# The order of the head in a one-core FFT mixing and expert routing kernel: o tiles, blank places, SyncE's queue, comparisons on GpSimd

## The chip, the core and the metric

The kernel runs on one core of a Trainium2 chip. A core has five engines with instruction streams of their own: TensorE (PE, with its weight loads shown as PEld), VectorE (DVE), ScalarE (ACT), GpSimd (POOL) and SyncE (SP), which here only issues transfers. Each engine works through its stream in order and waits at an instruction until what it needs has been signalled. The metric is the device time of one launch in microseconds; the number that counts is the median of several runs.

## What is computed

The input x has 8 batches of 2496 rows with 256 columns. Each batch goes through a real FFT along its rows, a multiplication with a filter and the inverse FFT. The 19968 resulting rows are tokens; each goes through the expert that a hash of its number names.

```python
def _attn_ref(x, filt_r, filt_i):
    X = np.fft.rfft(x, axis=1)
    F = (filt_r + 1j * filt_i)[None, :, :]
    y = np.fft.irfft(X * F, n=x.shape[1], axis=1)
    return y.astype(np.float32)

def _moe_ref(x, token_ids, w1, w2):          # E = 8 experts, D = 256, F = 1024
    expert_idx = token_ids * np.int64(2654435761) % np.int64(E)
    for e in range(E):
        mask = expert_idx == e
        h = np.maximum(x[mask] @ w1[e], 0.0)
        out[mask] = h @ w2[e]
```

## The kernel before

**FFT.** A batch of 2496 = 39 x 64 rows is transformed in three stages: DFTs of length 39 (stage 1), products with twiddles, the filter and back (stage 2, in 10 steps `u`, plus one that only finishes the last), and DFTs of length 39 again (stage 3). A step of stage 2 is `forward` (matmul pb on PE, then the products y and z on DVE: L263, L266 twice, L267) and, one step later, `back` or `back_c` (matmul pc on PE, copied by ACT). For batches 0 and 1 everything stays on the chip: `stage1_c` (L309), `turn2` (transposes, L319), `back_c` (L330), `turn4` (transposes, L345, the copy L349) and `stage3` (matmul pd, L219; copy to an o tile, L221). Batches 2 to 7 pass through DRAM between the stages: `stage1` writes d1 from ACT's queue (L242), `load2` reads it back in five groups of two transfers (L248).

**Routing.** The number of a token gives its expert at once, and from that its place in `xs`, a DRAM buffer of 163 tiles of 128 places, ordered so that each tile holds tokens of one expert. `count` and `route` work out the running numbers, `later(g)` for g = 1, 2, 3 compares them with the stages' limits (8 comparisons L544 and an addition L546 each), `places` sums them (L550), writes them to DRAM and reads them back as indices `sidx`. `tile_experts` and `experts` work out which expert each tile has; `weights` needs that (`chunk_i`). `blanks` works out the places that no token takes (at most 127 in an expert) and scatters rows of a blank tile to them (7 indirect transfers).

**Stage 3 and the scatter.** One call of `stage3` makes an o tile of up to four groups of rows, and each group goes out as one indirect transfer of POOL (`scatter`, L376), 22 for a batch. Before the copies DVE writes the token's number into the o tile (L363). The pool of o tiles has two buffers.

**Experts.** `step(i)` of the loop: gather tile i + 4 (L696, from SP), `up` (32 matmuls L715, relu on ACT and DVE into ht), fetch the next weights, `turn(i + 1)` (transposes L704, copy L706 on DVE), then the pieces of the FFT of later batches that are due, `down` (16 matmuls L727, copy L730), and the scatter of the results to the output (L731, POOL). The tiles fall into four stages; those of stage g hold tokens of batches below 2, 4, 6 and 8 only, so that the loop starts when batches 0 and 1 are in `xs`. What comes before the loop is called the head here.

**Order.** The order is written out by hand: `todo` is a list of pairs of a due time and a piece of work. It is sorted by due time; pieces below 0 make up the head, and pieces from 0 on run inside the step with that number. The due times are only an order: each engine receives its instructions in the order in which the pieces are called.

**Memory shared by turns.** `load1` puts x tiles 0 to 3 (batch 0's three, batch 1's first) into the quarters of the tile `wts`, all others into a pool of two buffers (tag x). `wts` later holds the weights of two experts (w1 and w2 of each in a quarter), and its first two and a half quarters hold batch 0's values between stage 2 and `turn4`. `rpool`, the routing's pool, is closed before the pools of the expert loop (`gath`, `work`, `outs`) are opened, so they take its room. `ppool` (tag p) has four buffers for y and z, given out in turn; `t4pool` has two.

Of the kernel before, what the change touches and what calls it, by code (L numbers as in the profile page):

```python
# [11 lines left out]
F32 = mybir.dt.float32  # L12
# [103 lines left out]
def kernel(  # L116
# [40 lines left out]
    chunk_i = keep.tile([1, 2, NT], I32)  # L157
    used_i = keep.tile([1, 1], I32)
    wf_t = cpool.tile([NR, NK], F32)
    wi_t = cpool.tile([NK, NR], F32)  # L160
# [15 lines left out]
    class Batch:  # L176
# [14 lines left out]
        def load1(self, v):  # L191

            k = self.b * NV + v
            if k < 4:
                xt = wts[0:NR, k, :].rearrange("p (j c) -> p j c", c=C)
            else:
                xt = xpool.tile([NR, XL, C], F32, name=f"x_{self.b}_{v}", tag="x")
            self.x[v] = xt

            n = min(XL, HN + 1 - XL * v)  # L200
            for h in range(H):
                nc.sync.dma_start(out=xt[h:NR:H, 0:n, :],
                                  in_=bass.AP(tensor=x.tensor, offset=x.offset + (self.b * S + H0[h] + XL * v) * C,
                                              ap=[[N2 * C, N1], [C, n], [1, C]]))
# [154 lines left out]
        def stage3(self, u):  # L359

            n = min(XG, HN + 1 - XG * u)
            o = opool.tile([NR, XG, W], F32, name=f"o_{self.b}_{u}", tag="o")
            nc.vector.tensor_scalar(o[:, 0:n, C:].bitcast(I32),  # L363
                                    tokno[:, XG * u:XG * u + n].unsqueeze(2).to_broadcast([NR, n, W - C]),
                                    float(self.b * S), None, op0=OP.add)
            v, half = divmod(u, XL // XG)

            copy = nc.scalar.copy if self.b < 2 else nc.vector.tensor_copy
            self.products(wi_t, (NK, 2 * NS), N1, self.t4[v][:, half * XG:half * XG + XG, :], o, copy, u, "pd")
            for i in range(n):  # L370
                j = XG * u + i
                r = NR if j < HN else N1
                scatter(o[0:r, i, :], sidx[0:r, self.b, j:j + 1], f"xs_{self.b}")
# [30 lines left out]
    rctx = ctx.enter_context(ExitStack())  # L404
    rpool = pool(rctx, "route", 1)
    nc.sync.dma_start(out=wf_t[:], in_=wf_dram.ap())
    for v in range(NV):
# [57 lines left out]
    def count():  # L465
# [4 lines left out]
        nc.vector.tensor_copy(eid[:], eid_i[:])  # L470
        mask = rpool.tile([P, E, NJ], F32)
        nc.vector.tensor_tensor(mask[:], eid[:].unsqueeze(1).to_broadcast([P, E, NJ]),
                                over(iota_e[:], NJ), op=OP.is_equal)
        maskf = mask[:].rearrange("p e j -> p (e j)")
        run = rpool.tile([P, E, NJ], F32)
# [18 lines left out]
    def route():  # L494
# [35 lines left out]
        nc.vector.tensor_scalar(thr[:], full[:, 0:G, :], float(TB), 1.0, op0=OP.mult, op1=OP.add)  # L530
        acc = rpool.tile([P, E, NJ], F32)
        tmp = mask
# [8 lines left out]
    def later(g):  # L541
        acc, tmp, run = rv["acc"], rv["tmp"], rv["run"]
        for e in range(E):
            nc.vector.tensor_scalar(tmp[:, e, :], run[:, e, :], rv["thr"][:, g, e:e + 1], rv["step"][:, g, e:e + 1],  # L544
                                    op0=OP.is_ge, op1=OP.mult)
        nc.vector.tensor_tensor(acc[:], acc[:], tmp[:], op=OP.add)  # L546

    def places():
        slot, slot_i = rv["eid"], rv["eid_i"]
        nc.vector.tensor_reduce(slot[:], rv["acc"][:].rearrange("p e j -> p j e"), axis=AX.X, op=OP.add)  # L550
        nc.vector.tensor_copy(slot_i[:], slot[:])
# [23 lines left out]
    def blanks():  # L575
# [20 lines left out]
                                       op0=OP.mult, op1=OP.add)  # L596
        at_i = rpool.tile([P, NQP], I32)
        nc.vector.tensor_copy(at_i[:], at[:])
        blank = tok[:].rearrange("p j two -> p (j two)")[:, 0:W]
        nc.gpsimd.memset(blank[:, 0:C], 0)  # L600
        nc.gpsimd.memset(blank[:, C:], N)
        for q in range(NQP):
            scatter(blank.bitcast(F32), at_i[:, q:q + 1], "xs_pad")

# [26 lines left out]

    def part2(b, at, ready=None):
        bt = batches[b]
        if b < 2:
# [20 lines left out]
    todo += [(t, lambda u=u: first.stage1_c(u)) for u, t in enumerate(spaced(-155, -151, NU))]  # L655
    todo += [(-154.9, count), (-152, route)]
    todo += [(t, lambda g=g: later(g)) for g, t in zip(range(1, G), (-148.1, -144.4, -140.8))]
    todo += [(-139, places), (-136.5, tile_experts), (-132, experts), (-128, blanks)]
    todo += [(t, lambda k=k: spread_filters(k)) for k, t in enumerate((-150.7, -146.6, -143, -137.6))]
    todo += [(t, lambda k=k: way_back(k)) for k, t in enumerate((-150.6, -146.5, -141.8, -137.5, -133.8))]  # L660
    todo += [(-150.4, lambda: first.turn2(0)), (-130.5, lambda: second.turn2(0))]
    todo += part2(0, spaced(-150, -130, N_2)) + part2(1, spaced(-130, -105, N_2))
    todo += [(t, lambda u=u: second.stage1_c(u)) for u, t in enumerate(spaced(-147.5, -132, NU))]
    todo += [(t - 2.6, lambda u=u: first.turn4(u)) for u, t in enumerate(spaced(-126, -104, NU))]
    todo += [(t - 2.6, lambda u=u: second.turn4(u)) for u, t in enumerate(spaced(-102, -82, NU))]
    todo += part3(0, spaced(-126, -104, NU)) + part3(1, spaced(-102, -82, NU))
    todo += [(-135, lambda: nc.sync.dma_start(out=wi_t[:], in_=wi_dram.ap()))]
    todo += part1(2, spaced(-101, -85, NU), [-128, -127, -126])
    todo += [(-99 + .1 * i, lambda i=i: (weights(i, 0), weights(i, 1))) for i in range(2)]

    todo += part1(3, spaced(2, 7, NU)) + part1(4, spaced(15, 20.5, NU))
    todo += part1(5, spaced(21, 27, NU)) + part1(6, spaced(36, 46, NU)) + part1(7, spaced(50, 60, NU))
    todo += part2(2, [-80, -77, -74] + spaced(.1, 5.5, N_2 - 3), -81) + part2(3, spaced(8.5, 15.5, N_2), 7)
    todo += part2(4, spaced(22, 31, N_2), 20.5) + part2(5, spaced(31.2, 46, N_2), 28)
# [7 lines left out]

    for _, piece in pre:
        piece()
    rctx.close()


    gath = pool(ctx, "gath", 8)
    work = pool(ctx, "work", 2)
    outs = pool(ctx, "outs", 3)  # L690
    xg, xt = {}, {}

    def load(i):
        q = tiles[i]
        xg[i] = gath.tile([P, W], F32, name=f"xg_{i}", tag="xg")
        ld = nc.sync.dma_start(out=xg[i][:], in_=xs[q * TB:(q + 1) * TB, :])  # L696
        for b in range(STAGES[stage_of[i]], B):
            tc.declare_no_dep(ld.ins, group=f"xs_{b}", reason="the tiles of a stage hold tokens of its batches alone")
        tc.add_to_no_dep_group("xs_read", ld.ins)

# [36 lines left out]

    for i in range(4):
        load(i)
    turn(0)  # L740
# [60 lines left out]
```

## Time and profile before

Three runs took 1574.37 to 1578.27 us, with a median of 1575.02 us. The profiled execution took 1594.02 us, and its span from the first to the last instruction is 1592.3 us.

| | busy us | share of the span | instructions |
|---|---|---|---|
| PE | 1503.4 | 94% | 9666 |
| PEld | 1375.8 | 86% | 9666 |
| DVE | 540.9 | 34% | 1029 |
| ACT | 233.2 | 15% | 401 |
| POOL | 344.3 | 22% | 359 |

| event in the head | us from the span's start |
|---|---|
| first matmul (x of batch 0 has landed) | 8.3 |
| last pc of batch 0 begins | 71.2 |
| first scatter of blank rows, first scatter of an o tile | 80.6, 90.6 |
| first weights issued | 143.0 |
| last scatter of batch 1 | 169.1 |
| first gather issued | 183.5 |
| first expert matmul | 189.6 |

A share of the whole span is an average over a head in which PE often waits and a loop in which it hardly does. So the head is read by itself: busy time in windows, then each engine's timeline, where the brackets give the idle time ahead of an instruction and what ended it.

### The profile page before, as it was taken

To read this page: it belongs to the slowest core of one execution; us is meant where nothing else is said; L and a number is where in the kernel's file an instruction comes from. 1 tells how busy PE (TensorE), PEld (TensorE's weight loads), DVE (VectorE), ACT (ScalarE), POOL (GpSimd) and SP (SyncE) were. 2 spreads that over 40 slices of the span, in tenths; PEclk is the share of its full clock that TensorE was granted. 3 is DMA by queue.
4 is the path that set the end of the run, shared out by engine and by line. 5 is a ranking of instruction groups with operands and counts; after the bars stand their busy time and mean duration, and the time that the engine had idled before them with its cause. 6 is when DMAs were issued, how large, how long until landed. Compare 5 with 4: busy or idle time off the path is not lost.

```text
span 1592.3 us, 26891 instructions
## 1 busy us (share of the span) xinstructions
PE 1503.4 (94%) x9666; PEld 1375.8 (86%) x9666; DVE 540.9 (34%) x1029; ACT 233.2 (15%) x401; POOL 344.3 (22%) x359
## 2 busy tenths in 40 slices
PE   6778499989999999999999999999999999999997
PEld 6766388979888999899989999899899999999997
DVE  6843342551244444334333433222212121212121
ACT  4443121111111111101111111000000000000000
POOL 0055101421320133112221223232211111111111
PEclk9989799999999999999999999999999999999999
DMA  8225647557764883574626744452426413122224
GB/s 223 69 70 185 218 144 227 176 168 213 235 216 150 244 260 120 173 221 138 201 90 204 236 127 136 121 156 78 135 68 220 146 42 114 62 92 88 90 89 136
DMA packets 144163, 242.03 MB, mean 152 GB/s; under 512 B 15356, under 2 KB 112559, under 8 KB 142157
## 3 DMA queue, kind: packets, MB, share of 16 engines
q1 hardware_dynamic: 104131, 165.30, 34.3%
q0 software_dynamic: 19120, 43.35, 8.1%
q10 hardware_dynamic: 20778, 31.64, 6.5%
q8 instruction: 79, 1.29, 0.3%
q14 instruction: 55, 0.45, 0.1%
HBM read 417.19 MB, written 75.08 MB: 309 GB/s over the span
## 4 chain that ended last, share of the span: by engine, by line
PE 87%; DVE 5%; DMA 3%; issue 2%; SPq 1%; ACT 1%; ACTq 0%; another core or an unknown queue 0%; POOL 0%; DVEq 0%; POOLq 0%
PE ups L715 35%; PE dps L727 34%; PE pd L219 4%; PE pb L257 4%; PE pc L279 3%; PE pa L219 3%; PE xps L704 2%; DVE z L266 2%; DMA xs<-o,sidx 1%; DMA d<-mid 1%; DVE y L263 1%; DVE y L267 1%; PE pa L309 1%; PE pc L330 1%; DMA xg<-xs 0%
## 5 line engine op out<-in xcount | busy, mean ns | idle before, releaser
L715 PEld LDWEIGHTS ups<-xt,wts 128*128 128x128 f32 x5088 | 594.5, 192 | 9.1 <-DVE xt L706 1.0
L715 PE MATMUL ups<-xt,wts 128*128 128x128 f32 x5088 | 595.2, 275 | 0.6 <-DVE xt L706 0.6
L727 PE MATMUL dps<-wts,ht 128*128 128x256 f32 x2544 | 580.3, 381 | 2.4 <-ACT ht L719 2.3
L727 PEld LDWEIGHTS dps<-wts,ht 128*128 128x128 f32 x2544 | 479.4, 191 | 68.2 <-ACT ht L719 3.3
L731 POOL DMA_INDIRECT out_dram<-osb,xg x159 | 155.9, 980 | 922.2 <-DVE osb L730 885.0
L721 DVE TENSOR_SCALAR ht<-ups 128x512 f32<-128x512 f32 x159 | 110.0, 692 | 522.9 <-PE ups L715 447.3
L719 ACT ACTIVATE ht<-ups 128x512 f32<-128x512 f32 x159 | 94.9, 597 | 1003.6 <-PE ups L715 777.8
L376 POOL DMA_INDIRECT xs<-o,sidx x176 | 176.0, 1000 | 240.1 <-DVE o L221 147.0
L730 DVE COPY osb<-dps 128x256 f32<-128x256 f32 x159 | 67.5, 425 | 396.1 <-PE dps L727 363.1
L266 DVE TENSOR_TENSOR z<-pb,filt 64x512 f32<-64x512 f32 x160 | 110.2, 689 | 2.3
L219 PE MATMUL pd<-t,wi_t 120*117 120x256 f32 x320 | 78.1, 388 | 2.1 <-DVE t L349 2.0
L263 DVE TENSOR_TENSOR y<-pb,filt 128x512 f32<-128x512 f32 x80 | 55.2, 690 | 60.7 <-PE pb L257 51.7
L279 PE MATMUL pc<-y,e_t 128*128 128x256 f32 x240 | 63.5, 387 | 10.1 <-DVE y L267 9.6
L257 PE MATMUL pb<-mid,d_t 128*128 128x256 f32 x240 | 64.3, 392 | 7.7 <-DMA mid<-d 7.7
L219 PEld LDWEIGHTS pd<-t,wi_t 120*117 120x117 f32 x320 | 57.2, 186 | 14.0 <-ACT o L221 2.8
L704 PE MATMUL xps<-ident,xg 128*128 128x128 f32 x326 | 62.7, 274 | 5.1 <-DMA xg<-xs 3.5
L706 DVE COPY xt<-xps 128x256 f32<-128x256 f32 x159 | 66.0, 415 | 2.6 <-PE xps L704 2.6
L279 PEld LDWEIGHTS pc<-y,e_t 128*128 128x128 f32 x240 | 45.1, 192 | 20.1 <-issue 6.6
L282 ACT COPY mid<-pc 128x512 f32<-128x512 f32 x60 | 35.1, 585 | 171.7 <-PE pc L279 161.0
L219 PE MATMUL pa<-x,wf_t 117*120 117x256 f32 x240 | 57.7, 385 | 2.5 <-DMA x<-in_x_dram 2.5
L257 PEld LDWEIGHTS pb<-mid,d_t 128*128 128x128 f32 x240 | 44.6, 197 | 15.0 <-issue 9.8
L267 DVE TENSOR_TENSOR y<-y,z 128x512 f32<-128x512 f32 x80 | 55.3, 692 | 2.7
(117 smaller groups left out, 513.3 us busy)
## 6 DMA issues: line engine op xcount, KB each, us to landing
wts<-in_moe_w_dram SPq DMA_DIRECT2D x322, 1024.0 KB
xg<-xs SPq DMA_DIRECT2D x163, 136.0 KB
mid<-d SPq DMA_DIRECT2D x60, 256.0 KB
d<-mid ACTq DMA_DIRECT2D x60, 256.0 KB
x<-in_x_dram SPq DMA_DIRECT2D x39, 312.0 KB
d<-mid ACTq DMA_DIRECT2D x12, 960.0 KB
t<-d SPq DMA_DIRECT2D x12, 960.0 KB
x<-in_x_dram SPq DMA_DIRECT2D x21, 234.0 KB
```

What stands on the lines that cost most here:

```text
L219: nc.tensor.matmul(out=ps[0:cols * H, k, :], lhsT=w[:], rhs=src[:, 2 * i + k, :], start=True, stop=True)
L257: nc.tensor.matmul(out=ps[:, i, :], lhsT=d_t[:, s, :], rhs=rhs, start=True, stop=True)
L266: nc.vector.tensor_tensor(out=z[b], in0=ps[a], in1=f_t[1][a, sl, :], op=OP.mult)
L267: nc.vector.tensor_tensor(out=y[:], in0=y[:], in1=z[:], op=OP.add)
L279: nc.tensor.matmul(out=ps[:, i, :], lhsT=e_t[:, 2 * u + i, :], rhs=pr[:, i, :], start=True, stop=True)
L376: st = nc.gpsimd.indirect_dma_start(out=xs[:], out_offset=bass.IndirectOffsetOnAxis(ap=index, axis=0), in_=rows, in_offset=None, bounds_ch ...
L704: nc.tensor.transpose(out=ps[:, dp, :], in_=xg[i][:, dp * P:(dp + 1) * P], identity=ident[:])
L715: nc.tensor.matmul(out=ps[:, k, :], lhsT=w1[:, dp, fp * P:(fp + 1) * P], rhs=xt[i][:, dp, :], start=(dp == 0), stop=(dp == DP - 1))
L719: nc.scalar.activation(out=dst, in_=ps[:], func=AF.Relu)
L721: nc.vector.tensor_scalar_max(dst, ps[:], 0.0)
L727: nc.tensor.matmul(out=ps[:, 0, :], lhsT=ht[:, fp, :], rhs=w2[:, fp, :], start=(fp == 0), stop=(fp == FP - 1))
L731: st = nc.gpsimd.indirect_dma_start(out=out[:], out_offset=bass.IndirectOffsetOnAxis(ap=xg[i][:, C:C + 1].bitcast(I32), axis=0), in_=o[:], ...
```

## The change

- `later(g)` runs on GpSimd instead of DVE, and its three calls come directly after `route`. The tiles `mask` and `acc` that it works on move from `rpool` into the two buffers of `t4pool`.
- The o tiles of batches 0 and 1 come alternately from the old pool and a new one of two buffers (`o2pool`), which ends with the routing's pool.
- `blanks` only works out the places and fills the blank tile (on DVE now, in a buffer of `ppool`); the scatters are a piece of their own, `pads`. Both come after stage 3 of batch 1. Gathers of the first three stages no longer depend on the blank places, which lie in the last stage.
- The first x tile of batch 2 goes into the fourth quarter of `wts`, so that its other two find the two pool buffers.
- `begin` closes the routing's pool, opens the loop's pools and issues the first four gathers, as a piece of the head: after the first two of batch 2's five reads and before two more. The fifth read, one of the three steps of batch 2's stage 2 and the first load of x of batch 3 move from the head into the first steps of the loop.
- Due times of `places`, `tile_experts`, `experts`, the turns and stage 3 shift a little.

```diff
@@ load1
-            k = self.b * NV + v
-            if k < 4:
+            k = self.b * NV + v if self.b < 2 else NV + NV * (self.b > 2) + v
+            if k <= NV:
                 xt = wts[0:NR, k, :].rearrange("p (j c) -> p j c", c=C)
@@ stage3
-            o = opool.tile([NR, XG, W], F32, name=f"o_{self.b}_{u}", tag="o")
+            o = (o2pool if self.b < 2 and u % 2 else opool).tile([NR, XG, W], F32, name=f"o_{self.b}_{u}", tag="o")
@@ count (acc in route alike)
-        mask = rpool.tile([P, E, NJ], F32)
+        mask = t4pool.tile([P, XL, C], F32, name="mask", tag="t4")[:].rearrange("p j c -> p (j c)")
+        mask = mask[:, 0:E * NJ].rearrange("p (e j) -> p e j", e=E)
@@ later
-            nc.vector.tensor_scalar(tmp[:, e, :], run[:, e, :], rv["thr"][:, g, e:e + 1], rv["step"][:, g, e:e + 1],
+            nc.gpsimd.tensor_scalar(tmp[:, e, :], run[:, e, :], rv["thr"][:, g, e:e + 1], rv["step"][:, g, e:e + 1],
                                     op0=OP.is_ge, op1=OP.mult)
-        nc.vector.tensor_tensor(acc[:], acc[:], tmp[:], op=OP.add)
+        nc.gpsimd.tensor_tensor(acc, acc, tmp, op=OP.add)
@@ blanks
-        blank = tok[:].rearrange("p j two -> p (j two)")[:, 0:W]
-        nc.gpsimd.memset(blank[:, 0:C], 0)
-        nc.gpsimd.memset(blank[:, C:], N)
+        blank = ppool.tile([P, 2 * C], I32, name="blank", tag="p")[:, 0:W]
+        nc.vector.memset(blank[:, 0:C], 0)
+        nc.vector.memset(blank[:, C:], N)
+        rv.update(blank=blank)
+
+    def pads():
         for q in range(NQP):
-            scatter(blank.bitcast(F32), at_i[:, q:q + 1], "xs_pad")
+            scatter(rv["blank"].bitcast(F32), at_i[:, q:q + 1], "xs_pad")
@@ order
-    todo += [(t, lambda g=g: later(g)) for g, t in zip(range(1, G), (-148.1, -144.4, -140.8))]
-    todo += [(-139, places), (-136.5, tile_experts), (-132, experts), (-128, blanks)]
+    todo += [(-154.9, count), (-152, route)] + [(-151 + .1 * g, lambda g=g: later(g)) for g in range(1, G)]
+    todo += [(-134, places), (-128, tile_experts), (-121, experts), (-83, blanks), (-81, pads)]
...
+    todo += [(-76, lambda: begin())]
...
-    todo += part2(2, [-80, -77, -74] + spaced(.1, 5.5, N_2 - 3), -81) + part2(3, spaced(8.5, 15.5, N_2), 7)
+    todo += part2(2, [-74, -73] + spaced(.1, 5.5, N_2 - 2), [-78, -77.9, -75, -74.5, .4]) + part2(3, spaced(8.5, 15.5, N_2), 7)
@@ begin, load
+    def begin():
+        nonlocal gath, work, outs
+        rctx.close()
+        gath, work, outs = pool(ctx, "gath", 8), pool(ctx, "work", 2), pool(ctx, "outs", 3)
+        for i in range(4):
+            load(i)
...
+        if stage_of[i] < G - 1:
+            tc.declare_no_dep(ld.ins, group="xs_pad", reason="places without a token lie in the last stage alone")
```

## The prediction

> **What bounds the kernel now.** I read the page's shares first (PE 94% of the span), then busy time by windows, the timeline and the waits of the head. From about 200 us the loop over the 163 expert tiles repeats with PE always busy: a tile costs 32 matmuls (3.57 us) and 16 (3.47), and PE never stands idle between 1300 and 1400 us. Before that it does:
>
> ```profile
> 80.00:120.00 40.00, 28.28 (x165) 25.00 (x164) 19.62 (x32) 16.34 (x29) 23.29 (x23) 0.87 0.22 72
> 120.00:160.00 40.00, 33.31 (x171) 26.38 (x170) 13.65 (x27) 14.95 (x29) 22.18 (x23) 0.91 0.61 190
> 160.00:200.00 40.00, 18.72 (x79) 13.98 (x80) 13.94 (x23) 3.99 (x9) 6.25 (x7) 0.74 0.62 209
> 200.00:240.00 40.00, 38.72 (x236) 35.13 (x235) 17.42 (x29) 8.13 (x14) 3.40 (x4) 1.00 0.48 153
> ```
>
> Columns: window and length, busy us of PE, its weight loads, DVE, ACT, POOL, then PE's clock, DMA share, GB/s. Between 160 and 200 us PE works less than half the time, at 0.74 of its clock. The change touches only this head and its seam to the loop. The first expert matmul starts at 189.62 us; all I forecast is how much earlier that is.
>
> Three holes, from the timelines of the single engines:
>
> ```profile
> 30.30 2.25 DVE L544 TENSOR_SCALAR mask<-run,thr,step 128x156 f32<-128x156 f32 x8
> 32.59 1.46 DVE L546 TENSOR_TENSOR acc<-acc,mask 128x1248 f32<-128x1248 f32 x1
> ...
> 97.42 0.58 ACT L221 COPY o<-pd 117x512 f32<-117x512 f32 x1 [1.35 <-remote]
> 101.07 0.58 ACT L221 COPY o<-pd 117x512 f32<-117x512 f32 x1 [3.06 <-issue]
> 105.38 0.58 ACT L323 COPY wts<-pt 128x512 f32<-128x512 f32 x1 [3.73 <-remote]
> 106.02 2.07 PE L257 MATMUL pb<-wts,d_t 128*128 128x256 f32 x4 [6.36 <-ACT wts L323]
> ...
> 150.83 2.94 PE L219 MATMUL pa<-x,wf_t 117*120 117x256 f32 x8 [2.53 <-DMA x<-in_x_dram]
> 154.49 1.07 ACT L221 COPY o<-pd 117x512 f32<-117x512 f32 x2 [7.92 <-DMA xs<-o,sidx]
> 169.08 0.90 POOL L376 DMA_INDIRECT xs<-o,sidx  x1 [0.30 <-issue]
> 188.38 0.66 PE L704 MATMUL xps<-ident,xg 128*128 128x128 f32 x2 [3.46 <-DMA xg<-xs]
> 189.62 5.25 PE L715 MATMUL ups<-xt,wts 128*128 128x128 f32 x32 [0.59 <-DVE xt L706]
> ```
>
> The number in brackets is the idle time before an instruction and what ended it. (1) Up to 72 us DVE is the busiest engine (35.9 of 40 us), and PE waits for its y. (2) From 94 to 112 us ACT, and behind it PE, stand still. (3) After 147 us x of batch 2, o tiles and transfers hold everything.
>
> **Comparisons to GpSimd.** They leave DVE: 3 x (8 comparisons, 2.25, + 1.46) = 11.1 us. PE's batch 0 stage 2 runs from 23.5 to 72.4 us with 10.2 us of waits, nearly all for y; that is the ceiling. Going through it matmul by matmul, PE becomes the bound, and one wait stays: the reduction of the places (2.44 + 0.24) still stands before y of step 9. That gives about 8. On GpSimd the nearest row is its 128x128 affine_select, 0.29 us: by columns 0.35 for 156, 24 x 0.35 = 8.5 us; it has no row with two inputs. Here the Trainium skill speaks against the move ("GPSIMD Engine Reference", Engine selection): GpSimd is about twice as slow for two-input elementwise work, about line rate for one input. By it the adds cost 3 x 2 x 1.46 = 8.8 us, together about 17, from 19.8 to 37 us; at twice DVE's price throughout, 22. The places are needed at about 59 us, so both answers hide. A second rule bites: "SBUF — State Buffer", Who interferes with whom, says a DVE instruction with two SBUF inputs is blocked for the whole of a GpSimd instruction that reads SBUF. By the rows alone DVE pays nothing; by the rule each y<-y,z add (one per step, 0.69) may wait for a comparison (0.35) or an add (2.9): at most 3 x 2.9 + 7 x 0.35 = 11, all of the gain. No run here shows it. I take 2, since the adds fill half of GpSimd's 17 us, and PE hides part. Net **-6** (ends 0 and -9). The tile numbers' pieces (1.5 + 1.4 us of DVE, 0.6 of PE) only move later, onto similar ground; their result is needed at about 105.
>
> **Pads last, four o tiles.** POOL's 7 scatters of blanks (80.6 to 90.2) stood ahead of the first o tile, whose rows were ready at 81.3. With two o tiles the third copy then waits for the first's scatters: 1.35 us on ACT. Without both, that goes. But the next waits on ACT, 3.06 and 3.73, name no o tile; the trace gives no releaser. PE idles 1.66 + 6.36 + 3.05 = 11.1 us here, and runs at half clock after it (4.1 us for two groups that take 2.1). So this piece is worth between -2 (only the o tile's share) and -13 (all). The trace puts the first late copy right behind the o tile's release and can't say whether it sets off the rest, so I take about the middle: **-6**.
>
> With stage 3 of batch 1 the bound changes. A scatter takes 1.295 us of POOL, four of them 5.2 us an o tile; PE needs 1.73 + 0.87 + 1.73 = 4.35 us for the stage 1, turn and stage 3 of a step. So POOL sets the pace, and four tiles suffice to hide a landing (94.46 to 97.45: about 2 us after issue). Batch 1's first scatter was at 132.52; 12 us earlier is 120.5. Its 22 take 28.5: done at **149**, against 170. This takes in hole 3: the 7.9 and 2.6 us waits for o tiles and the 2.53 for x go, but POOL lets PE keep only part.
>
> **x of batch 2 and weights.** The third x load waited 70.6 us for a tile that batch 2 itself had to read first (the longest of the waits in SP's queue, and the first line below: us in total, times, longest), with four weight loads behind it (the first and last of them):
>
> ```profile
> SPq L202 <- PE pu L345: 70.6, 1, 70.6
> ```
>
> ```profile
> 142.99 0.00 SPq L399 DMA_DIRECT2D wts<-in_moe_w_dram  x1
> 155.02 0.39 SPq L401 DMA_DIRECT2D wts<-in_moe_w_dram  x1
> ```
>
> Now the first goes to a free quarter of the weights' tile and all three are read by about 60. The weights then wait for batch 0's turn back (123 us, now about 111), and the last of them for stage 1 of batch 2 to read its first x. They land by about 125, so DMA isn't at 1.0 when batch 2's stage 1 writes out (that landing took 9.8 us, a quiet one 4) and when the last scatters land. New behind SP's last weight load is nothing until batch 2's reads at about 143.
>
> **The seam.** SP issued ten reads of batch 2 (8.84 us) and x of batch 3 (2.55) before the gathers; the chain of waits has the first tile's landing as the last transfer ahead of the loop:
>
> ```profile
> 183.48 4.76 DMA xg<-xs
> ```
>
> Now four reads precede them, x of batch 3 goes out during the first tile (its stage 1 still comes two tiles on), and the gathers wait for batch 1's scatters: 149 + 2 = 151, landing 4.8 later, 156, plus transpose. But a new wait comes in. The blank rows now lie in the pool of y and z, four buffers in turn: blank, y, z of step 0, y of step 1, and then **z of step 1 takes the blank's buffer**. It cannot be written until the seven pad scatters have read it: 149 + 7 x 1.28 + 2 = 160. Behind it on DVE stand y's add and the copy of the first expert tile, so: 160 + 1.39 + 0.69 + 0.42 + hand-overs 0.3 = 162.8, first expert matmul about **163**, against 189.6: -26.6. The ten small instructions of the blanks (2.2 us) and two fills run on an idle DVE. One step of batch 2 (8 matmuls, 1.7 us) moves behind the seam into the loop, where PE is full: +1.7. **Sum -25.**
>
> The loop itself keeps its work. The profiled execution took 1594.02 us (span 1592.3), 19 us more than the median 1575.02; I take the same 25 off both: about 1569 and **1550**. If those 19 us are partly stalls of the head that timed runs lack, the gain shrinks; that is in the range.
>
> **Rivals.**
> - *The stall at 94 us goes whole, and GpSimd blocks nothing* (0.22): -9, -13 in place of -6, -6: 22 us rather than 12 before POOL's pace sets in: about 1540. For it: the stall follows the first o wait. Against: 3.06 and 3.73 us without a releaser.
> - *Landings, not POOL, set the seam* (0.24): weights and x pulled forward fall on batch 0's and 1's scatters; one landing of 11.8 us (the one from 142.56 in the chain) instead of 2 delays o tiles or pads by 10: about 1560, and 1564 where the ACT stall stays too (-2 for -6). For it: DMA share 1.0 when the weights load. Against: four tiles give 15 us of slack.
> - *GpSimd too slow* (0.04), slower than before: the places wait for the comparisons, and behind their reduction DVE, in order, holds batch 0's last y and with it everything up to the seam. Every us by which the comparisons end after 59 is lost; the gain of 25 is gone when they end at 84, that is (84 - 19.8 - 8.8)/24 = 2.3 us for each of the 24, nearly seven times the row's 0.35. At 3 us they end at 100.6: 16.6 slower, about 1592.
> - *Nothing moves* (0.02): POOL or SP is held by something else as long; 1575.
>
> The likeliest case (0.48) has 1543 to 1557 by the ends of its own unknowns, taken together only in part. The range 1535 to 1564 takes in most of the first two rivals. A difference under 0.3% (4.7 us) can't be told from none: faster 0.94, same 0.02, slower 0.04.
>
> **What the new profile would show.** Comparisons on POOL from 19.8 to 37-45 us; last batch 0 pc near 66 rather than 72; no ACT wait for scatters of o; scatters of o before those of blanks, the latter from 149 to 158; weights issued near 111; z of batch 2 released by the blank's scatter; first expert matmul at 163. Wrong: comparisons over 1 us each, y adds several times 0.69 us, or an ACT standstill of 10 us that has only moved; or a first expert matmul on time and the gain lost again in the loop's waits.

## The result, and the profile after

The changed kernel took 1564.18 us in the median (1562.16 to 1564.86, four runs); the kernel before, run beside it, took 1574.69. The ratio is 0.9926, with an interval of 0.9909 to 0.9944: faster by some 10.5 us, where 25 were forecast, and 0.2 us past the upper end of the range. The profiled execution took 1562.16 us, with a span of 1560.4.

First the windows of the changed kernel, with the same columns as before (us of PE, its weight loads, DVE, ACT, POOL, then PE's clock, DMA share, GB/s):

```profile
80.00:120.00 40.00, 37.40 (x239) 32.77 (x238) 27.51 (x52) 21.91 (x40) 23.50 (x24) 1.00 0.53 176
120.00:160.00 40.00, 25.78 (x118) 20.04 (x117) 10.99 (x31) 11.63 (x22) 27.52 (x28) 0.81 0.80 248
160.00:200.00 40.00, 34.63 (x197) 30.92 (x196) 20.22 (x32) 6.72 (x12) 1.94 (x2) 0.89 0.33 112
200.00:240.00 40.00, 39.59 (x248) 36.15 (x247) 13.03 (x22) 9.08 (x16) 3.88 (x4) 1.00 0.71 208
```

The hole that lay between 160 and 200 us has moved into the window ahead of it. Next a selection from the timelines of the single engines in the head, in order of time:

```profile
18.33 9.06 POOL L549 TENSOR_SCALAR mask<-run,thr,step 128x156 f32<-128x156 f32 x8 [16.04 <-DVE acc L542]
...
49.51 2.84 POOL L551 TENSOR_TENSOR acc<-acc,mask 128x1248 f32<-128x1248 f32 x1
49.93 2.97 DVE L268 TENSOR_TENSOR y<-y,z 128x512 f32<-128x512 f32 x1
...
64.38 2.42 DVE L555 TENSOR_REDUCE eid<-acc 128x156 f32<-128x1248 f32 x1
69.99 2.07 PE L331 MATMUL pc<-e_t,y 128*128 128x128 f32 x8 [4.25 <-DVE y L268]
...
118.69 0.99 POOL L377 DMA_INDIRECT xs<-o,sidx  x1 [2.45 <-ACT o L222]
...
145.88 0.89 POOL L377 DMA_INDIRECT xs<-o,sidx  x1 [0.30 <-issue]
153.45 3.75 PE L258 MATMUL pb<-mid,d_t 128*128 128x256 f32 x8 [10.43 <-DMA mid<-d]
154.80 0.97 POOL L377 DMA_INDIRECT xs<-blank,at_i  x1 [0.30 <-issue]
161.18 1.39 DVE L267 TENSOR_TENSOR z<-pb,filt 64x512 f32<-64x512 f32 x2 [2.11 <-DMA xs<-blank,at_i]
163.81 6.10 PE L729 MATMUL ups<-xt,wts 128*128 128x128 f32 x32 [2.90 <-DVE xt L720]
```

The comparisons now stand on POOL and end at 52.35; one y add beside them takes 2.97 us. Batch 1's 22 scatters are issued from 118.69 to 145.88 with 0.30 us, or little more, between one and the next. A z of batch 2 waits 2.11 us for the last blank rows, and the loop starts at 163.81. SP's longest wait for x and its first and last weight load before the loop:

```profile
SPq L203 <- ACT wts L324: 33.7, 1, 33.7
```

```profile
101.35 0.43 SPq L400 DMA_DIRECT2D wts<-in_moe_w_dram  x1
...
125.60 0.39 SPq L402 DMA_DIRECT2D wts<-in_moe_w_dram  x1
```

In the chain of waits the last transfer ahead of the loop is no longer a gather but the last of the blank rows:

```profile
154.80 6.26 DMA xs<-blank,at_i
...
163.81 6.10 PE ups L729 x32
```

### The profile page after: what moved, and what is told of

It is laid out like the page before. It is cut to its first block, busy times and chain, and to the rows that moved or that the text cites. A ratio compares the mean times of both kernels' runs of the same rounds, so it can differ in the third digit from the quotient of the medians.

```text
span 1560.4 us, 26888 instructions
## 1 busy us (share of the span) xinstructions
PE 1495.8 (96%) x9666; PEld 1374.9 (88%) x9666; DVE 533.0 (34%) x1004; ACT 234.2 (15%) x401; POOL 376.3 (24%) x384
## 4 chain that ended last, share of the span: by engine, by line
PE 91%; DVE 4%; DMA 2%; issue 2%; SPq 1%; POOL 1%; ACT 0%; ACTq 0%; POOLq 0%; DVEq 0%
PE ups L729 36%; PE dps L741 35%; PE pd L220 4%; PE pb L258 4%; PE pc L280 3%; PE pa L220 3%; PE xps L718 2%; DVE z L267 1%; PE pc L331 1%; DMA d_t<-d_tbl 1%; DVE y L268 1%; POOL xs L377 1%; DVE y L264 1%; PE pt L320 1%; SPq L203 0%
## 5 line engine op out<-in xcount | busy, mean ns | idle before, releaser
L729 PEld LDWEIGHTS ups<-xt,wts 128*128 128x128 f32 x5088 | 595.3, 192 | 11.5 <-DVE xt L720 3.3
L258 PE MATMUL pb<-mid,d_t 128*128 128x256 f32 x240 | 64.6, 394 | 10.4 <-DMA mid<-d 10.4
L220 PE MATMUL pa<-x,wf_t 117*120 117x256 f32 x224 | 52.9, 379 | 0.0
```

What stands on the lines that cost most here:

```text
L220: nc.tensor.matmul(out=ps[0:cols * H, k, :], lhsT=w[:], rhs=src[:, 2 * i + k, :], start=True, stop=True)
L258: nc.tensor.matmul(out=ps[:, i, :], lhsT=d_t[:, s, :], rhs=rhs, start=True, stop=True)
L729: nc.tensor.matmul(out=ps[:, k, :], lhsT=w1[:, dp, fp * P:(fp + 1) * P], rhs=xt[i][:, dp, :], start=(dp == 0), stop=(dp == DP - 1))
```

## The experiments

Every run stands beside runs of the kernel before on the same chip. These runs showed something that one number can't be read without: chips differ. Where the kernel before takes 1575 to 1578 us, I call the chip of the first kind, where it takes 1597 or 1598, of the second. Chips 7 and 8 were of the first kind (chip 8 in two sessions 48 minutes apart), chips 5 and 10 of the second. Which chip the prediction's profile came from is not on record.

| run | edit against the changed kernel | before, us | this, us | ratio and interval | first expert matmul, us |
|---|---|---|---|---|---|
| first kind | | | | | |
| b_again | the kernel before | 1577.32 | 1577.38 | 0.9999 (0.9986 to 1.0011) | 181.26 |
| (result) | none | 1574.69 | 1564.18 | 0.9926 (0.9909 to 0.9944) | 163.81 |
| after_3 | none | 1577.70 | 1566.84 | 0.9930 (0.9907 to 0.9952) | 163.73 |
| after_5 | none | 1577.80 | 1564.30 | 0.9918 (0.9902 to 0.9934) | 165.54 |
| no_gps | comparisons on DVE | 1577.32 | 1567.78 | 0.9937 (0.9920 to 0.9954) | 168.19 |
| no_gps_2 | comparisons on DVE | 1577.70 | 1567.53 | 0.9944 (0.9926 to 0.9963) | 167.68 |
| two_o | two o tiles | 1577.32 | 1567.10 | 0.9939 (0.9922 to 0.9956) | 166.00 |
| stall_back_2 | two o tiles, blanks first | 1577.80 | 1568.08 | 0.9943 (0.9920 to 0.9965) | 168.47 |
| old_seam | gathers after the whole head | 1577.32 | 1564.21 | 0.9914 (0.9898 to 0.9931) | 168.06 |
| gather_first_2 | gathers ahead of batch 2's reads | 1577.70 | 1560.69 | 0.9896 (0.9875 to 0.9917) | 153.90 |
| gather_places | the same, places a step later | 1577.70 | 1555.73 | 0.9856 (0.9833 to 0.9879) | 151.71 |
| second kind | | | | | |
| after_again | none | 1597.24 | 1577.78 | 0.9876 (0.9858 to 0.9893) | 177.08 |
| after_4 | none | 1597.88 | 1579.06 | 0.9907 (0.9873 to 0.9941) | 172.69 |
| pads_early | blanks first | 1597.24 | 1586.16 | 0.9933 (0.9919 to 0.9947) | 182.06 |
| pads_early_2 | blanks first | 1597.88 | 1583.04 | 0.9925 (0.9898 to 0.9953) | 178.33 |
| stall_back | two o tiles, blanks first | 1597.88 | 1588.85 | 0.9944 (0.9921 to 0.9967) | 183.98 |
| old_x | x of batch 2 in the old buffers | 1597.24 | 1584.21 | 0.9912 (0.9894 to 0.9930) | 180.29 |
| old_x_2 | x of batch 2 in the old buffers | 1597.88 | 1584.73 | 0.9921 (0.9894 to 0.9949) | 182.98 |
| gather_first | gathers ahead of batch 2's reads | 1597.24 | 1575.25 | 0.9861 (0.9843 to 0.9878) | 162.60 |

### The same kernels again: which execution was forecast from?

The kernel before, unedited, and the changed one, unedited.

> The kernel before, unchanged, in another execution. Theory A (the profile I predicted from was not a typical execution: its head held about 19 us of stalls that other runs lack): span near 1573 us, first expert matmul near 171 us instead of 189.6, ACT without the idle of 3 to 4 us ahead of single copies between 92 and 106 us; the loop after it takes about 1402 us as in the first profile. Theory B (the head is the same in every execution and the 19 us lie in the loop): first expert matmul near 189 us again, loop near 1384 us.

> The changed kernel itself, beside the three that follow, on one chip. Theory A (the gain is what the head of an ordinary execution could give, some 17 us at the seam less 3 us of work moved into the loop): ratio 0.991 to 0.994. Rival (part of the gain seen so far is another chip's): 0.995 or above.

> The changed kernel once more, as the measure for the three that follow on the same chip. Theory A (there are two kinds of chips here: on one the kernel before takes about 1576 us and the change brings 10 to 12 us, on the other about 1597 and the change brings 18 to 20, because there some engines stand still for 3 to 7 us at a time in the head, in both kernels): if the kernel before takes about 1576, ratio 0.992 to 0.994 and no idle without a releaser over 1 us on ACT, DVE or PE between 60 and 165 us; if it takes about 1597, ratio 0.986 to 0.989 and several of them. Rival (the gain varies from run to run, whatever the chip): no such pairing.

> The changed kernel as the base for stall_back_2 on the same chip: ratio 0.992 to 0.994 where the kernel before takes about 1577 us, 0.986 to 0.991 where it takes about 1597.

> The changed kernel again, as the base for the other three on the same chip: ratio 0.992 to 0.994 where the kernel before takes about 1577 us, 0.986 to 0.989 where it takes about 1597.

Here are ACT's waits in the loop (window 200 to 1600 us; engine and line, what was waited for, us in total, times, longest), first in the profile that the prediction used, then in b_again, the same kernel:

```profile
ACT ht L719 <- PE ups L715: 770.2, 125, 9.7
...
ACT ht L719 <- issue: 136.6, 22, 9.7
```

```profile
ACT ht L719 <- PE ups L715: 954.7, 154, 9.3
ACT mid L282 <- PE pc L279: 157.7, 55, 4.9
```

In the first, 22 waits of ACT have no releaser that the profile shows; in b_again that line is absent. It is a mark of that profile, not the cost: ACT waits ahead of ht 158 times for 996 us in all there, 157 times for 970 us in b_again, so most of the 22 are its usual waits for PE, with no releaser named. The loop took 1592.3 - 189.62 = 1402.7 us there and 1574.8 - 181.26 = 1393.5 in b_again, and the head 189.6 against 181.3. So 9.1 of the 17.5 us between the two spans lie in the loop and 8.4 in the head, and neither of the two theories stated ahead of b_again holds alone. In the loop PE, its bound, was busy 5.3 us longer there for the same 8900 matmuls (1372.7 against 1367.4) and idle 3.8 us longer. The changed kernel has the same two faces: no such wait in its first profile, and on chips of the second kind the first of these lines (after_4, in the loop), with standstills in the head such as these two (after_again, timelines):

```profile
ACT ht L733 <- issue: 132.0, 20, 9.7
```

```profile
116.88 0.69 ACT L333 COPY mid<-pc 128x512 f32<-128x512 f32 x1 [5.18 <-remote]
152.11 0.75 DVE L353 COPY t<-pu 120x256 f32<-120x256 f32 x2 [7.43 <-remote]
```

The prediction's profile is thus like those of the second kind, and its 1594.02 us lies within that kind's runs of the kernel before (1591.55 to 1600.69), while the median it was subtracted from is of the first (no run of it over 1582.35). The change brings 10.5, 10.9 and 13.5 us on the first kind and 19.5 and 18.8 on the second. What makes the engines stand still there was not found; the packets that load instructions are as many in both profiles (79 and 55 on their two queues).

The first expert matmul of b_again can be set against the result's, 17.45 us earlier. Its own marks, from the timelines of PE and POOL:

```profile
73.23 1.13 PE L330 MATMUL pc<-e_t,y 128*128 128x128 f32 x8 [1.20 <-DVE y L267]
...
101.05 1.13 PE L257 MATMUL pb<-wts,d_t 128*128 128x256 f32 x4 [1.31 <-ACT wts L323]
102.65 1.13 PE L330 MATMUL pc<-e_t,y 128*128 128x128 f32 x8 [0.47 <-DVE y L267]
...
122.59 0.99 POOL L376 DMA_INDIRECT xs<-o,sidx  x1 [0.92 <-ACT o L221]
...
157.76 0.90 POOL L376 DMA_INDIRECT xs<-o,sidx  x1 [0.30 <-issue]
181.26 6.39 PE L715 MATMUL ups<-xt,wts 128*128 128x128 f32 x32 [0.58 <-DVE xt L706]
```

PE's wait behind ACT near 100 us, 6.36 us in the profile of the prediction, is 1.31 here, though the code is the same.

### Comparisons back on DVE

The edit, shortened:

```diff
-            nc.gpsimd.tensor_scalar(tmp[:, e, :], run[:, e, :], ...
+            nc.vector.tensor_scalar(tmp[:, e, :], run[:, e, :], ...
-        nc.gpsimd.tensor_tensor(acc, acc, tmp, op=OP.add)
+        nc.vector.tensor_tensor(acc, acc, tmp, op=OP.add)
-    [(-151 + .1 * g, lambda g=g: later(g)) for g in range(1, G)]
+    [(t, lambda g=g: later(g)) for g, t in zip(range(1, G), (-148.1, -144.4, -140.8))]
```

> The changed kernel with the comparisons back on DVE at their old due times. Theory A (DVE was the bound of batch 0's stage 2 and POOL's scatters set the end): 6 us of the gain are lost at batch 0's last pc, which comes near 72 us again, and the time is 1568 to 1571. Rival (GpSimd's comparisons hold the places as long as they relieve DVE): within 1.5 us of 1564.

> The changed kernel with the comparisons on DVE at their old due times, beside the changed kernel on one chip. Theory A (they cost PE some 4 us of batch 0's stage 2: 47.5 us there with, 43.3 without them, and the rest of the head moves along): 3 to 5 us slower than the changed kernel. Rival (POOL's scatters and batch 2's landing take it up): within 1.5 us.

Groups of instructions by line between 18 and 72 us (busy us, mean ns of one | idle before), of the changed kernel and then of no_gps:

```profile
L549 POOL TENSOR_SCALAR mask<-run,thr,step 128x156 f32<-128x156 f32 x24 | 24.8, 1044 | 16.2 <-DVE acc L542 16.0
...
L268 DVE TENSOR_TENSOR y<-y,z 128x512 f32<-128x512 f32 x10 | 9.3, 929 | 0.3
```

```profile
L268 DVE TENSOR_TENSOR y<-y,z 128x512 f32<-128x512 f32 x9 | 6.2, 691 | 0.3
```

A comparison takes 1.04 us on GpSimd in the mean of 24. Most take 0.87 to 0.89; five are longer (0.96 to 2.98), the longest of them beside DVE's last accumulation. All of it is hidden: the last addition ends at 52.35, the reduction of the places begins at 64.38. The price on DVE is 10 x (0.929 - 0.691) = 2.4 us on the y adds. Batch 0's stage 2 takes 47.48 us in no_gps and 49.86 in no_gps_2, against 43.25 to 44.31 in the three traces of the changed kernel on the first kind. In the traces the first scatter of batch 1 stands at 122.51 in no_gps_2 and 118.76 in after_3, 3.8 us earlier, and the spans (1564.9 and 1561.1) differ by as much. The medians differ by only 0.7, and the intervals lie over each other: after_3's six runs spread from 1562.33 to 1568.47, and the longer of them have a lower granted clock (0.981 to 0.983 against 0.987 to 0.988). no_gps is 3.5 us slower than after_5, the changed kernel on the same chip 48 minutes later; these intervals overlap too. The traces say some 4 us, as expected ahead of no_gps_2; the times can't confirm it.

### Blank rows first, two o tiles: the term that missed

The edits, shortened:

```diff
-            o = (o2pool if self.b < 2 and u % 2 else opool).tile(
+            o = opool.tile(
-    (-83, blanks), (-81, pads)]
+    (-127.95, blanks), (-127.9, pads)]
-        blank = ppool.tile([P, 2 * C], I32, name="blank", tag="p")[:, 0:W]
-        nc.vector.memset(blank[:, 0:C], 0)
+        blank = tok[:].rearrange("p j two -> p (j two)")[:, 0:W]
+        nc.gpsimd.memset(blank[:, 0:C], 0)
```

two_o has the first edit alone, pads_early the other two, stall_back all three.

> The changed kernel with one pool of two o tiles for all batches. Theory A (with the pads out of the way two tiles cover a landing of 2 to 3 us, POOL at 5.2 us an o tile stays the pace): within 2 us of 1564. Rival (the o tiles were the stall): ACT waits for scatters of o in batch 1's stage 3 with several us each, and the time is 1569 to 1574.

> The changed kernel with the blank rows scattered at their old place, ahead of the first o tile, from the routing's own tile. Theory A (POOL has some 8 us of idle time between batch 0's o tiles and makes up for the 9 us before batch 1 ends; DVE's wait of 2.1 us for the blank's buffer goes): within 2 us of the changed kernel. Rival (pads first delay every later scatter): last scatter of batch 1 some 8 us later, 6 to 8 us slower.

> Blank rows scattered ahead of the first o tile again, four o tiles. On the other chip this cost 8.4 us with a standstill of 7.87 us on ACT in its trace. If the standstill is the chip's and not the order's, then where the kernel before takes about 1577 us this is 0 to 3 us slower than the changed kernel; if the order itself costs, 7 to 9 us.

> The whole second part of the change undone: blank rows scattered ahead of the first o tile, and two o tiles. If the term of 6 us that the forecast gave this part was too large only because its profile came from a chip on which ACT also stands still without a releaser, then on a chip where the kernel before takes about 1577 us this kernel is no more than 3 us slower than the changed one, and from the last pc of batch 0 to batch 1's first scatter it takes 49 to 51 us (48.7 in the changed kernel). If the term was right and something else ate it, the kernel is 6 us slower or more and this stretch takes about 55 us. On a chip where the kernel before takes about 1597 us both mix with the standstills.

> Blank rows ahead of the first o tile and two o tiles, as in stall_back, which took 9.8 us more than the changed kernel where the kernel before took 1598 us. Where the kernel before takes about 1577 us: 0 to 3 us slower than the changed kernel if that cost was the chip's standstills, 6 or more if the order itself costs it; the stretch from the last pc of batch 0 to batch 1's first scatter 49 to 51 us or about 55.

On the second kind stall_back is 9.8 us slower than after_4 on its chip (the intervals overlap; the first expert matmul of its trace is 11.3 us later), and its stretch from the last pc of batch 0 to batch 1's first scatter takes 66.2 us against 54.8. Its timelines hold the standstill that the prediction had looked at, with PE behind it:

```profile
102.90 0.69 ACT L333 COPY mid<-pc 128x512 f32<-128x512 f32 x1 [7.97 <-remote]
...
103.65 2.07 PE L258 MATMUL pb<-wts,d_t 128*128 128x256 f32 x4 [6.68 <-ACT mid L333]
```

On the first kind stall_back_2 is 3.8 us slower than after_5 (the intervals overlap), and ACT's long waits in this stretch, apart from those for PE, are for o tiles (4.09, 2.86 and 3.75 us); the first is

```profile
99.69 1.07 ACT L222 COPY o<-pd 117x512 f32<-117x512 f32 x2 [4.09 <-DMA xs<-o,sidx]
```

The same stretch as a window, in b_again, stall_back_2, after_5 and the changed kernel's first profile, one fence each (length, busy us of PE and weight loads, DVE, ACT, POOL; PE's clock):

```profile
73.23:122.59 49.36, 44.11 (x275) 38.56 (x276) 32.63 (x65) 25.61 (x47) 30.00 (x29) 1.00 0.24 77
```

```profile
70.53:125.28 54.75, 48.37 (x287) 41.58 (x288) 34.64 (x72) 25.61 (x47) 32.16 (x34) 0.96 0.54 175
```

```profile
70.39:120.70 50.31, 47.59 (x279) 41.47 (x279) 31.68 (x60) 25.79 (x47) 24.45 (x26) 0.92 0.54 172
```

```profile
69.99:118.69 48.70, 45.44 (x278) 39.90 (x279) 31.58 (x60) 25.81 (x47) 24.44 (x25) 0.97 0.54 177
```

PE's idle time is length less busy: 5.2, 6.4, 2.7 and 3.3 us. So the part takes some 2 to 2.5 us of waits away against the kernel before, and 3.7 against itself undone. But PE's busy time in the changed kernel is 1.3 to 3.5 us longer than in b_again. Its clock is below 1.00 in all three kernels with the new order, and they have in common that PE has just waited 4.25 us at the head of this stretch: the first eight matmuls after that wait take 2.07 us, against 1.13 in b_again, and the granted clock is 0.50 from 69.6 to 73.0 us. b_again has such a dip too, but within batch 0's stage 2 (0.50 from 50.1 to 53.5 us, behind a wait of 2.82), so part of this is a cost that has changed its stretch. after_5 has a second dip near 116 us. The pieces of the tile numbers (0.6 us of PE) came into the stretch as well. Of the two readings stated ahead neither holds in full: the stretch is not "49 to 51 us" with the part undone but 54.75, as the second had it, and the kernel is neither within 3 us nor 6 slower, but 3.8. The marks say where the rest went. With the part undone the stretch is 4.4 us longer than in after_5, and batch 1's scatters, issued over 30.78 us rather than 27.29, 3.5 longer; but from the last of them to the first expert matmul it takes 12.41 us rather than 17.55, because no blank rows stand there.

two_o alone: ACT waits for o tiles again (70 to 180 us),

```profile
ACT o L222 <- DMA xs<-o,sidx: 10.5, 3, 4.5
```

and batch 1's 22 scatters are issued over 30.46 us instead of 27.19. The last of them is issued at 148.48, only 2.6 us later than in the result, but stage 2 of batch 0 had begun 3.1 us earlier in this trace. So two tiles do not cover a landing here, against the first theory; in the times it doesn't show, as 0.9939 can't be told from 0.9918. pads_early is 8.4 us slower than after_again and pads_early_2 4.0 slower than after_4; only the first pair's intervals lie apart. Both have standstills of ACT (7.87 and 6.54 us) without a releaser, and neither ran on the first kind, so the size of the blank rows' place alone is open there.

### x of batch 2 in its old buffers

```diff
-            k = self.b * NV + v if self.b < 2 else NV + NV * (self.b > 2) + v
+            k = self.b * NV + v
```

> The changed kernel with x of batch 2 in the old buffers, so that its third load waits for batch 2's own stage 1 and the weights wait behind it. Theory A (in an ordinary execution this is the largest part: the wait for x of 4.3 us on PE, and weights that collide with stage 1's output and the scatters): first weights near 125 us instead of 101, first expert matmul 5 to 9 us later, 6 to 9 us slower than the changed kernel. Rival (POOL's scatters at 5.2 us an o tile set the seam in any case): within 2 us of it.

> x of batch 2 in the pool of two buffers again, weights behind it. If the transfers collide by themselves, it is 4 to 8 us slower than the changed kernel here too (6.4 on the other chip), with x and weights issued between 130 and 150 us and batch 2's first matmul of stage 2 waiting for a landing; if only that chip's standstills made it so, 0 to 2.

6.4 and 5.7 us slower than the changed kernel on the same chip; the intervals of the first pair lie just apart (0.9893 and 0.9894), those of the second overlap. In old_x, SP's wait is back and the first weights go out at 142.06, and batch 2's first matmul of stage 2 waits longer for its reads (below, after after_again's on the same chip):

```profile
SPq L203 <- PE pd L220: 69.7, 1, 69.7
```

```profile
165.61 3.75 PE L258 MATMUL pb<-mid,d_t 128*128 128x256 f32 x8 [6.64 <-DMA mid<-d]
```

```profile
172.02 3.75 PE L258 MATMUL pb<-mid,d_t 128*128 128x256 f32 x8 [16.62 <-DMA mid<-d]
```

Both runs fell on the second kind; what it is worth on the first is not shown.

### The seam: old order, and gathers first

old_seam calls `begin` after the whole head, with all ten reads and three steps of batch 2 and the first load of x of batch 3 ahead of it. gather_first goes the other way, and gather_places moves the places too:

```diff
@@ gather_first
-    part2(2, [-74, -73] + spaced(.1, 5.5, N_2 - 2), [-78, -77.9, -75, -74.5, .4])
+    part2(2, spaced(.1, 5.5, N_2), [-74, -73.9, -73.8, -73.7, 1.1])
@@ gather_places, besides
-    (-134, places)
+    (-131.9, places)
```

> The changed kernel with the seam as before: all five reads of batch 2 and the first load of x of batch 3 ahead of the gathers, three steps of batch 2 in the head. Theory A: the gathers are issued some 8 us later (six more reads and three x loads at 0.4 to 0.9 us each), of which one step (1.7 us) comes back in the loop: 1568 to 1571. Rival (the blank's buffer holds DVE anyway and hides the reads): 1563 to 1566.

> The changed kernel with the first four gathers ahead of batch 2's reads, and all of batch 2's stage 2 in the loop. Theory A (at the seam PE waits for batch 2's stage 1 to land, 10.4 us, while the first expert tile only needs the scatters, done 2 us earlier, and DVE's wait for the blank's buffer no longer stands ahead of it): first expert matmul near 155 us instead of 163.8, two more steps of 1.7 us in the loop: 4 to 6 us faster than the changed kernel. Rival (gathers wait as long for scatters as the reads do for their data): within 1.5 us of it.

> Gathers ahead of batch 2's reads, all of its stage 2 in the loop, beside the changed kernel. Theory A (two steps more in the loop, 3.5 us, against an expert loop that starts 9 us earlier): 4 to 6 us faster than the changed kernel. Rival (what the head loses, the loop pays: its steps are slowed at the start by cold PE and landings): within 2 us.

> As gather_first, and the reduction of the places one step later, behind y of batch 0's last step. Theory A (PE's wait of 4.2 us for that y, which stood behind the reduction of 2.7 us on DVE, shrinks to 1.5, and the head moves along): 1.5 to 3 us faster than gather_first. Rival (the indices come later and hold the first scatters instead): same or slower; first scatter of an o tile later than 82.5 us.

old_seam's first expert matmul is 4.3 us later than the result's and 2.5 later than after_5's (the same chip), but its median, 1564.21 us, is that of after_5. One step of batch 2 is behind it when the loop starts; yet in the traces its loop is only 0.7 us shorter than the result's (1395.9 and 1396.6) and 0.9 shorter than after_5's. So the earlier gathers of the change bring nothing that the times show, as the rival had it. In gather_first_2 neither batch 2 nor the blank rows stand ahead of the first tile; it waits for nothing but its gather:

```profile
152.67 0.66 PE L718 MATMUL xps<-ident,xg 128*128 128x128 f32 x2 [7.05 <-DMA xg<-xs]
...
153.90 5.81 PE L729 MATMUL ups<-xt,wts 128*128 128x128 f32 x32 [0.57 <-DVE xt L720]
```

That is 9.8 us before after_3's. In the two profiled executions only 1.7 are left of it, in the medians 6.1 (the intervals just overlap): the loop took 1405.5 us against 1397.4, since it now has 12 matmuls of batch 2 more in it and PE's half clock behind the wait falls partly into it (0.50 to 158.1 and again from 164.9 to 168.3 us). On the second kind gather_first is 2.5 us faster than after_again, which can't be told from none. gather_places then takes away most of the wait of 4.25 us at the end of batch 0's stage 2, though not the slow matmuls behind it:

```profile
67.99 1.85 PE L331 MATMUL pc<-e_t,y 128*128 128x128 f32 x8 [1.82 <-DVE y L268]
...
150.47 0.66 PE L718 MATMUL xps<-ident,xg 128*128 128x128 f32 x2 [8.34 <-DMA xg<-xs]
151.71 3.57 PE L729 MATMUL ups<-xt,wts 128*128 128x128 f32 x15 [0.57 <-DVE xt L720]
```

At 1555.73 us it beats both kernels: 11 us under the changed one and 22 under the one before, with intervals apart from both. Its share of 5 us over gather_first_2 is less sure (0.9856 and 0.9896, intervals just overlapping).

## Why the prediction was right and wrong

The sum step by step, in the prediction's own stretches; measured is b_again against the result's profile, both on the first kind:

| step | forecast | measured |
|---|---|---|
| start to first pb of batch 0 | 0 | 25.48 to 26.74: +1.3 |
| batch 0's stage 2, first pb to last pc | -6 | 47.75 to 43.25: -4.5 |
| on to batch 1's first scatter | -6 | 49.36 to 48.70: -0.7 |
| batch 1's 22 scatters, to the end of the last | -9.0 | 36.07 to 28.08: -8.0 |
| from there to first expert matmul | -5.6 | 22.60 to 17.04: -5.6 |
| loop | +1.7 | 1393.5 to 1396.6: +3.1 |
| sum | -25 | -14.4 |

**The step that failed** is the one from batch 0's last pc to batch 1's first scatter, the "-6" for pads last and four o tiles (with ends at -2 and -13), and under it the sentence "I take the same 25 off both". The prediction saw two waits of ACT without a releaser (3.06 and 3.73 us), let half of them hang on the o tile, and booked the gain against a median from a chip that doesn't have them: PE's waits there are 1.31 and 0.47 us in b_again, not 11.1. So the result's stretch is 0.7 us shorter than b_again's (after_5's is 0.9 longer), which is 5.3 of the 10.6 us that this pair of profiles is short of the sum. On the second kind the part measures 9.8 us in stall_back (intervals overlapping), the order of what the profile promised. On the first it measures 3.8 against itself undone (overlapping too), and next to nothing is left in this stretch against the kernel before, because the changed order adds PE time there. The change's whole gain on the second kind, 19.5 and 18.8 us, is 6 short of the 25; on the first it is 11.5 to 14.5 short. The text named this danger ("if those 19 us are partly stalls of the head"), and two signs were at hand: the profiled execution lay 16 us above the slowest timed run (1594.02 and 1578.27), and 136.6 us of waits had no releaser in the loop, where next to nothing changed.

**Comparisons.** The term was 1.5 us too large, and its mechanism held only in part. PE's idle time in this stretch fell by 1.9 us (10.4 to 8.5), where the sum had some 6; of the 10.2 us of waits that it called "nearly all for y", 1.05 were for ACT's e_t and 1.61 for DVE's `past`. The other 2.6 us came off PE's busy time: 0.6 for the tile numbers, which moved on, and the rest with its clock, which was 0.96 in b_again and 1.00 in the result, as the dip now lies behind the last pc, in the next stretch. Another 1.3 us went with a later start. First pb lies between 23.5 and 26.8 us in these traces, and moves with the pace of PE's first matmuls: some 0.22 us each, twice the 0.11 of later ones, until about 18.4 us in the result, 16.0 in b_again and 11.7 in the prediction's profile.

GpSimd's price was missed (0.35 forecast, 0.88 for most and 1.04 in the mean), just above the mark of 1 us that the prediction set for itself as wrong, and stayed hidden. What the lock of the shared port costs was met: 2 forecast, 2.4 measured, nearly all on one add of 2.97 us: it began at 49.93, and ended at 52.90, 0.55 us after the GpSimd addition beside it (52.35). The Trainium skill's rule ("SBUF — State Buffer", Who interferes with whom) is borne out for that addition. For the comparisons it isn't seen on DVE's side: of the eight that follow each other here, the first ran from 41.50 to 42.39, and the y add that began within it took its usual time (that at 46.24, begun within another, as well).

```profile
41.50 7.93 POOL L549 TENSOR_SCALAR mask<-run,thr,step 128x156 f32<-128x156 f32 x8
42.13 0.69 DVE L268 TENSOR_TENSOR y<-y,z 128x512 f32<-128x512 f32 x1
```

The comparisons next in turn took 1.78 and 0.96 us rather than 0.88, which suggests that here GpSimd was the one that waited; times on POOL are rough.

The wait on PE that was to stay, behind the places' reduction, stayed, at 4.25 us, where 10.2 less 8 leaves 2.2; the dip of PE's clock behind it was not in the sum.

**POOL's pace, the seam.** 28.5 us were forecast for the scatters, and 28.4 went by from batch 1's first to the first of the blank rows (118.69 to 147.07), with no gap on POOL; the new wait of z for the blank rows came as described (2.11 us), and the first expert matmul at 163.8 against 163. This meeting is partly chance, though: it was reckoned down from 189.6, not from 181.3, batch 1's first scatter was at 118.7 rather than 120.5, and the blank rows took 14.0 us to the last landing rather than 11.0 (that landing came 6.3 us after issue), so that two misses cancelled.

**x and weights.** Weights were issued from 101 to 126 us, earlier than forecast, and batch 2's reads began at 148.92 rather than 143. As the blank rows landed later still, this decided nothing.

**Rivals.** The time lies at the upper end of what "landings set the seam" gave (1560 to 1564), but what that rival describes is seen only in small: the last blank rows landed 6.3 us after issue and so held the seam some 3 us longer than reckoned, not 10, and no scatter of batch 1 waited for an o tile's landing. GpSimd did not become too slow: its comparisons would have had to end 12 us later to delay the places at all.

**The rest of the loop's +3.1** beyond the moved step is not explained. The medians differ by 10.5 us where these two profiled executions differ by 14.4: the changed kernel's was the fastest of its four, 2.0 us under their median, and b_again's lay 1.9 us above the median beside the result (1576.54 and 1574.69).

## What to carry to other kernels

Where the profiled execution lies outside the range of the timed ones, as 1594 us did above 1574 to 1578, profile again before forecasting: a gain from stalls that the timed runs don't have can't be subtracted from their median. Waits without a releaser in a part that the change leaves alone were a second sign here, but such a wait can also be an ordinary one whose releaser the profile doesn't name, so compare the sum of all waits, and ask whether the bound waits behind them. Give a stall to the change only as far as its releaser is named. A step that feeds the pace of the next stage is placed as late as its consumer allows, ahead of nothing that PE waits for: here the places one step later and the gathers ahead of batch 2 together brought as much again as the change itself (11.1 us, intervals apart).

## What the runs showed of the hardware

- Two kinds of chips, as far as five sessions on four chips show: the same kernel takes 1577 us on one and 1597 on the other. On the second kind the trace has 17 to 22 waits of ACT without a releaser in the loop and standstills of ACT or DVE of up to 8.5 us in the head; in the five traces with the blank rows last, ACT always stands still at the same copy (L333, near 115 us) for 4.6 to 5.2 us. The eleven traces of the first kind show no wait without a releaser over 1 us in the head, and none ahead of ht in the loop. The cause is open.
- A comparison with two scalars per partition, 128x156, takes 0.88 us on GpSimd when nothing holds it, and 0.28 on DVE (2.25 for eight). The Trainium skill ("GPSIMD Engine Reference", Engine selection) has one-input work there at about line rate; here it is 3.1 times slower (3.7 with the waits in the mean of 1.04), and the measurement decides. Two-input additions took 2.9 us against 1.46, twice as long, as that page says.
- PE's clock dips behind short waits. Where a wait of 4.25 us ends batch 0's stage 2, eight matmuls took 2.07 us rather than the 1.13 that they take behind a wait of 1.20, with a granted clock of 0.50 for the 3.4 us from 69.6 on: the wait costs more than its length. A shorter wait was no sure cure: behind 1.82 us in gather_places they took 1.85 us, and behind 2.82 us in b_again 2.05.
